# Two PSUM tiles in place of one for the score maxima of a mixture-of-experts and attention kernel, and more of the maxima beside the second layers

## The chip, the cores and the metric

The kernel runs on one core of a Trainium2 chip. The core has TensorE (matrix products, written to PSUM, a memory of 8 banks of 512 fp32 values in each of 128 partitions), VectorE, ScalarE and GpSimd (elementwise work and reductions), SyncE (here it starts most DMAs) and its DMA engines. The metric is the device time of one execution in microseconds.

## The reference

Two blocks read the same normalised input and are added to the input.

```python
x = A_x                                  # 1 x 2048 x 448
xn = layernorm(x)
return x + A(xn) + B(xn)

def A(x):                                # 16 query heads, one key and value head, Dh = 28
    q = (x @ wq).reshape(...)            # 16 heads of 28
    k, v = x @ wk, x @ wv                # 2048 x 28
    p = softmax(q k^T * 28 ** -0.5)
    return (p v) @ wo

def B(x):                                # 8 experts, each token uses 2
    gates = softmax(x @ wg); top 2, weights normalised over the two
    h = gelu(x @ w1[e])                  # 448 -> 1792
    y = h @ w2[e]                        # 1792 -> 448
    return the weighted sum over the two experts
```

For a stable softmax the kernel needs, for each query and head, the maximum of its scores over the 2048 keys. That maximum is taken ahead of the attention, while the experts run.

## The kernel before, in words

**Order of the work.** First come the norms, the projections and the gate; then the eight experts, sorted by how many tokens they have (capacities of 576 to 512, CAPS, line 25); then the attention. Expert 1 (e = 0 in the code) has its own loop (lines 1077 to 1172). Experts 2 to 8 (e = 1 to 7, lines 1224 to 1374) are the ones that the change is about. In their part the order of TensorE's instructions is the order of the program; the queues of the other engines are laid out by a scheduler, which puts the work marked as high priority first.

**An expert.** Its tokens' rows are gathered and turned by TensorE transposes (turn_x, line 268: four transposes into one PSUM bank, then two ScalarE copies out of it, then two GpSimd subtractions for the low halves). Every fp32 operand is split into a high and a low part, and a product is three products of these. The first layer (first_layer, line 1241) goes over 14 half pieces of w1 with 22 matrix products each, 11 into either half of a bank; ScalarE applies the gelu. In the second layer (lines 1286 to 1360) TensorE's rows are used as four groups of 32: in each of four phases there are 14 x 3 = 42 steps of four products (line 1338), one per row group, into the accumulators acc[0] to acc[3]; phases are parted by a drain of TensorE (line 1331). acc[0] and acc[1] are the one-bank tiles ps_w, acc[2] and acc[3] the halves of the two-bank tile ps_s2. At the end four copies (lines 1353 to 1360), alternately by ScalarE and VectorE, take the accumulators out; the turned rows of the next expert (two sets at the start of the layer, two or three at its end) and, for experts 2 to 5, the products of the tokens beyond 512 (line 1367) follow.

**The maxima.** A unit is one query tile of 128, one head and two blocks of 512 keys that lie 1024 keys apart. Units 0 to 447 cover query tiles 2 to 15. Its maximum is taken from two products: D (D_of, line 1188), queries times the difference of the two key blocks, and B (B_of, line 1198), queries times the second block. max(a, b) = relu(a - b) + b: ScalarE writes the Relu of D to a buffer (line 1322), and VectorE adds B, in place, and reduces by the maximum (pair_max, line 1203). There are two places for units:

- A burst in the first layer (pair_burst, line 1205; called from due, line 1231, ahead of the third product of a half piece's second half): two units by D and B in the four-bank tile ps_s, and a third one by its two key blocks in the tile ps_s2, reduced by VectorE at once (line 1220). Experts 2 to 7 have 8 bursts in 14 calls, expert 8 has 10. Where a call has no burst, it may finish a query tile (s_last, line 132).
- A round in the second layer (maxima, line 1310): D of two new units into banks 0 and 1 of the tile ps_s (ps in the code), and B of the two units of the round before into banks 2 and 3; then the two Relus of the new units and the two maxima of the old ones. The Relus go to two pairs of buffers in turn, RR: the two halves of cp, or two buffers gf. A round is issued before the first step and after steps 8, 17, 25, 34 and 42 of every phase, as long as the queue has units. Experts 2 to 7 take 40 units here (20 rounds of new units and one for the last maxima), expert 8 takes the rest.

The pool of these tiles is psM (line 892): ps_s with four banks, ps_s2 with two, ps_w0 and ps_w1 with one each, which fills PSUM. Expert 1 uses ps_s as well, in s_burst (line 151): up to seven units of another form, four of them reduced in one instruction of VectorE from the four banks (line 179); and turn_first (line 781) and first_scores (line 1038) put single sets there.

Of the kernel before, what the change touches and what calls it, by code (L numbers as in the profile page):

```python
# [86 lines left out]
def moe_attention(ctx, tc, x, wq, wk, wv, wo, wg, w1, w2, out, hp=200, slow=0.4, first=0.9, fin=11, find=4):  # L87
    nc = tc.nc
# [62 lines left out]
    def s_burst(b0, n):  # L151


        p, p2 = bank["s"]()
        p3 = other_psum() if n > 6 else None
        for i in range(n):
            t, c, g, j = (b0 + i) // 64, (b0 + i) // 16 % 4, (b0 + i) // 4 % 4, (b0 + i) % 4
            if (b0 + i) % 64 == 32 and t + 1 < NT:
                s_query(t + 1)
            r = slice(32 * j, 32 * j + DH)  # L160
            k = i - (n > 6)
            nc.tensor.matmul(p3 if k < 0 else p[:, k, :] if k < 4 else p2[:, k - 4, :], SQ[t][r, g, :],
                             kT4[r, c * 512:(c + 1) * 512], start=True, stop=True)
        cp = mp.tile([128, 2, 512], F32, name="cp", bufs=1)
        with tc.high_priority(offset=hp):
            parts = [(0, p3[:, None, :])] if n > 6 else []
            k = len(parts)
            parts.append((k, p[:, 0:min(n, 4)]))
            if n - k > 4:
                nc.scalar.activation(cp[:, 0:n - k - 4], p2[:, 0:n - k - 4], AF.Copy)  # L170
                parts.append((k + 4, cp[:, 0:n - k - 4]))
            red = None
            for k, q in parts:

                o, m = (b0 + k) % 192, q.shape[1]
                l = min(m, 192 - o)
                for o, a, z in ((o, 0, l), (0, l, m)):
                    if a < z:
                        r = V.tensor_reduce(MX[0][:, o:o + z - a], q[:, a:z], axis=AX.X, op=OP.max)
                        if red:  # L180
                            order(r.ins, red)
                        red = r.ins.name
# [99 lines left out]
    with ExitStack() as p0:  # L282
# [498 lines left out]
        def turn_first(i):  # L781
# [3 lines left out]
            if i < 2:  # L785
                p = psP.tile([128, 512], F32, name="ps_t", bufs=3)
            else:
                p = (psM.tile([128, 4, 512], F32, name="ps_s", bufs=1) if i % 2 == 0 else s2_psum())[:, 0]
            p = GT[i] = p.rearrange("p (c n) -> p c n", c=4)[:, :, 0:n]
# [130 lines left out]

    bank["s"] = lambda: (psM.tile([128, 4, 512], F32, name="ps_s", bufs=1), s2_psum())
    bank["s"]()
# [115 lines left out]
    def first_scores():  # L1038

        p = bank["s"]()[0]  # L1040
        mm = products([p[:, j] for j in range(4)], att["q"], 0)
        trail.append(mm.ins.name)
        P = att["P"] = att["p"].tile([128, 4, 512], F32, name="Pf", bufs=1)
        for j in range(0, 4, 2):
            order(nc.scalar.activation(P[:, j:j + 2], p[:, j:j + 2], AF.Exp, scale=SCALE).ins, trail[-1])

# [158 lines left out]
    def pair_burst():  # L1205
        u = UD[0]
        UD[0] += 3
        p, p2 = bank["s"]()
        D_of(u, p[:, 0])
        D_of(u + 1, p[:, 1])  # L1210
        ask(u + 2)
        key_of(u + 2, 0, p2[:, 0])
        B_of(u, p[:, 2])
        B_of(u + 1, p[:, 3])
        key_of(u + 2, 1, p2[:, 1])
        cp = mp.tile([128, 2, 512], F32, name="cp", bufs=1)
        m = pair_at(u + 2)[-1]
        with tc.high_priority(offset=hp):
            nc.scalar.activation(cp, p[:, 0:2], AF.Relu)
            V.tensor_reduce(MX[0][:, m:m + 1], p2.rearrange("p a b -> p (a b)"), axis=AX.X, op=OP.max)  # L1220
            for k in range(2):
                pair_max(u + k, cp[:, k], p[:, 2 + k])

    for e in range(1, E):
# [6 lines left out]
        def due(e=e):  # L1231
            k = slots[0]
            slots[0] += 1
            n = 10 if e == E - 1 else 8
            if (k + 1) * n // 14 > k * n // 14:
# [49 lines left out]

        ps = psM.tile([128, 4, 512], F32, name="ps_s", bufs=1)
        for i, *a in XS:
            turn_x(e + 1, i, *X[e + 1], *a, ps[:, 2 + i])
        XS = []
# [10 lines left out]

        until = UD[0] + 40 if e + 1 < E else NU
        queue = list(range(UD[0], until, 2))
# [7 lines left out]
        def maxima():  # L1310
# [4 lines left out]
            for j in range(4):  # L1315
                for u, what, o in ((old, B_of, 2), (new, D_of, 0)):
                    if u is not None and u % 4 // 2 == j // 2:
                        what(u + j % 2, ps[:, o + j % 2])
            with tc.high_priority(offset=hp):
                for k in range(2):  # L1320
                    if new is not None:
                        nc.scalar.activation(ra[k], ps[:, k], AF.Relu)  # L1322
                for k in range(2):
                    if old is not None:
                        pair_max(old + k, rb[k], ps[:, 2 + k])
            old = new

        maxima()
        for ph in range(4):
            if ph:  # L1330
                nc.tensor.drain()
            for f in range(NF):
                a, b = (w[:, f % 2, :] for w in W2[e, f // 2])
                for i, (l, w) in enumerate(((0, a), (1, a), (0, b))):
# [5 lines left out]
                    step = f * 3 + i + 1  # L1340
                    if step in (8, 17, 25, 34, 42):
                        if step < 42:
# [6 lines left out]
        for k, (i, *a) in enumerate(XS):  # L1349
            turn_x(e + 1, i, *X[e + 1], *a, ps[:, k])  # L1350
        r = sum(CAPS[:e])
        YY = [GP[0].tile([128, 2, 512], F32, name="yy", tag="g0", bufs=7) for _ in range(2)]
        for k in range(4):
            y = YY[k // 2][:, k % 2, 0:D]
            with tc.high_priority(offset=hp):
                if k % 2:
                    V.tensor_copy(y, acc[k][:, 0:D])
# [344 lines left out]
```

## Time and profile before

| | us |
|---|---|
| median of 3 runs (lowest, highest) | 1604.8 (1598.74, 1606.59) |
| the profiled execution | 1602.6 |
| its span, first to last instruction | 1600.9 |
| TensorE busy in the span | 1401.8 (88%) |
| ScalarE busy | 1014.8 (63%) |
| VectorE busy | 887.3 (55%) |
| GpSimd busy | 622.9 (39%) |
| second layer of expert 2: from, to | 243.7, 306.3 |
| second layers of experts 3 to 7, length | 62.2 to 62.8 |
| attention, from 1064 to 1600 | 536.0, TensorE busy 519.8 |

The profile is one execution. A line of the timeline has the start in us, the duration in us, the engine, the line of the program, the operation, what it writes and reads by the program's names (ps_s stands for every tile whose name begins so, ps_s2 among them), the shapes and how many such instructions were merged; in brackets stand the engine's idle time before it and what ended it. Lines of waits have the waiting group, whom it waited for, the total in us, the number of times and the longest. Lines of groups have the busy time and the mean in ns behind the bar, then idle time. PE is TensorE (PEld its weight loads), ACT ScalarE, DVE VectorE and POOL GpSimd.

### The profile page before, as it was taken

The page shows a single profiled execution, that of the slowest core. Times are in us where ns is not written, and L with a number is a line of the kernel's source. Part 1 is how long each engine was busy: PE and PEld are TensorE (multiplying, and loading weights), DVE is VectorE, ACT ScalarE, POOL GpSimd, SP SyncE. Part 2 cuts the span into 40 slices and gives each one's busy share as a digit, 9 for nine tenths or more (in the row PEclk, how much of TensorE's full clock was granted, in tenths as well). Part 3 has the DMA queues.
Part 4 walks back from the last instruction along what each step waited for, and adds up shares of the span by engine and source line. Part 5 has one row for each costly group of instructions (what it writes and reads, how often), then busy time and mean ns, then how long its engine had stood idle before and what let it go on. Part 6 is the DMA issues. An engine that isn't in the chain of part 4 may idle for free. (4 is left out here: it accounts for less than half of the span.)

```text
span 1600.9 us, 35307 instructions
## 1 busy us (share of the span) xinstructions
PE 1401.8 (88%) x14325; PEld 990.5 (62%) x14325; DVE 887.3 (55%) x1655; ACT 1014.8 (63%) x1275; POOL 622.9 (39%) x556
## 2 busy tenths in 40 slices
PE   7989997797698788779779779789999999999997
PEld 6877786586576567668668668554444444444443
DVE  7888873363444436337337338446555555555554
ACT  6645564365355446347447446449798999899985
POOL 7244483175157138118218217101432243224323
PEclk9999999899999989999999999999999999999999
DMA  8931241133023124114114113211121212111211
GB/s 261 306 110 39 61 135 49 55 96 91 27 80 115 33 65 133 40 43 135 47 55 135 47 55 98 51 57 32 43 67 49 55 44 67 49 54 45 67 38 37
DMA packets 103331, 122.72 MB, mean 77 GB/s; under 512 B 15298, under 2 KB 91506, under 8 KB 103038
## 3 DMA queue, kind: packets, MB, share of 16 engines
q1 hardware_dynamic: 98078, 104.11, 21.7%
q0 software_dynamic: 5088, 16.32, 3.8%
q8 instruction: 114, 1.87, 0.5%
q14 instruction: 51, 0.42, 0.1%
HBM read 96.67 MB, written 23.72 MB: 75 GB/s over the span
## 5 line engine op out<-in xcount | busy, mean ns | idle before, releaser
L1510 ACT ACTIVATE P<-ps_s 128x1536 f32<-128x1536 f32 x255 | 356.1, 1449 | 45.2 <-PE ps_s L1034 45.2
L1203 DVE CUSTOM_DVE_ANT_0 cp<-ps_s,cp 128x512 f32<-128x512 f32 x254 | 164.9, 686 | 179.9 <-ACT gf L1322 172.2
L1338 PE MATMUL ps_s<-w2h,gg 32*128 32x448 f32 x1568 | 250.9, 378 | 2.0 <-issue 1.0
L1540 PE MATMUL ps_s<-P,vaug 128*32 128x512 f32 x2040 | 249.2, 602 | 1.9 <-DVE P L1525 0.9
L1338 PE MATMUL ps_w<-w2h,g 32*128 32x448 f32 x1568 | 247.2, 375 | 1.0
L228 POOL TENSOR_TENSOR w1l<-st,w1h 128x1024 fp32r<-128x1024 f32 x49 | 120.7, 2464 | 266.8 <-ACT w1h L61 266.3
L76 PE MATMUL ps_w<-xeh,w1h 128*128 128x256 f32 (+2 forms) x896 | 170.4, 302 | 5.2 <-ACT gf L1256 4.9
L1338 PEld LDWEIGHTS ps_s<-w2h,gg 32*128 32x128 f32 x1568 | 162.0, 192 | 7.1 <-issue 6.3
L1196 PE MATMUL ps_s<-kT,qs 28*128 28x512 f32 x506 | 111.0, 456 | 60.9 <-DVE mx L1203 60.9
L1338 PEld LDWEIGHTS ps_w<-w2h,g 32*128 32x128 f32 x1568 | 160.1, 192 | 3.7 <-issue 3.1
L1322 ACT ACTIVATE gf<-ps_s 128x512 f32<-128x512 f32 x136 | 74.0, 596 | 136.2 <-PE ps_s L1191 98.4
L1338 PE MATMUL ps_s<-w2l,gg 32*128 32x448 f32 x784 | 155.4, 372 | 0.0
L1191 PE MATMUL ps_s<-kd,qs 28*128 28x512 f32 x390 | 99.7, 503 | 61.2 <-DVE mx L1203 49.4
L1338 PE MATMUL ps_w<-w2l,g 32*128 32x448 f32 x784 | 153.2, 370 | 0.0
L76 PEld LDWEIGHTS ps_w<-xeh,w1h 128*128 128x128 f32 x896 | 132.9, 192 | 32.4 <-issue 21.6
L1203 DVE CUSTOM_DVE_ANT_0 gf<-ps_s,gf 128x512 f32<-128x512 f32 x136 | 88.6, 689 | 114.0 <-ACT cp L1322 113.2
L1220 DVE TENSOR_REDUCE mx<-ps_s 128x1 f32<-128x1024 f32 x58 | 70.8, 1221 | 145.5 <-PE ps_s L1196 145.5
L1322 ACT ACTIVATE cp<-ps_s 128x512 f32<-128x512 f32 x138 | 75.0, 595 | 120.4 <-PE ps_s L1196 100.7
L76 PE MATMUL ps_w<-xeh,w1l 128*128 128x256 f32 (+2 forms) x896 | 149.9, 290 | 0.0
L1034 PEld LDWEIGHTS ps_s<-qah,kT 29*128 29x128 f32 x1024 | 72.5, 183 | 122.5 <-issue 77.7
L1548 DVE TENSOR_TENSOR o<-ps_s,o 128x512 f32<-128x512 f32 x111 | 76.8, 691 | 122.7 <-PE ps_s L1540 122.7
L1034 PE MATMUL ps_s<-qah,kT 29*128 29x512 f32 x1024 | 138.0, 457 | 3.9 <-DVE o L1548 3.7
(316 smaller groups left out, 3129.1 us busy)
## 6 DMA issues: line engine op xcount, KB each, us to landing
st<-in_B_w_dram SPq DMA_DIRECT2D x56, 448.0 KB
st<-in_B_w_dram SPq DMA_DIRECT2D x52, 384.0 KB
st<-in_B_w_dram SPq DMA_DIRECT2D x104, 64.0 KB
y_d<-yy SPq DMA_DIRECT2D x28, 224.0 KB
xn_d<-xn SPq DMA_DIRECT2D x16, 256.0 KB
rb<-s_d SPq DMA_DIRECT2D x15, 256.0 KB
xn<-in_A_x_dram SPq DMA_DIRECT2D x16, 224.0 KB
qs<-qh_d SPq DMA_DIRECT2D x64, 56.0 KB
```

The lines of the kernel that those rows point to most:

```text
L76: yield nc.tensor.matmul(out, a, b, start=i == 0, stop=i == n - 1)
L228: (nc.gpsimd if e else V).tensor_tensor(b, st, a.bitcast(F32), op=OP.subtract)
L1034: mm = nc.tensor.matmul(ps[j], k[r, ks], q[r].rearrange("p h q -> p (h q)"), start=i == 0, stop=i == 2)
L1191: nc.tensor.matmul(bank, q, KD[0][r, c * 512:c * 512 + 512], start=True, stop=True)
L1196: nc.tensor.matmul(bank, q, kT4[r, o:o + 512], start=True, stop=True)
L1203: V.tensor_tensor_reduce(d, b, d, 1.0, -3.0e38, OP.add, OP.max, MX[0][:, m:m + 1])
L1220: V.tensor_reduce(MX[0][:, m:m + 1], p2.rearrange("p a b -> p (a b)"), axis=AX.X, op=OP.max)
L1322: nc.scalar.activation(ra[k], ps[:, k], AF.Relu)
L1338: mm = nc.tensor.matmul(acc[k][:, 0:D], gate(k, f, l)[r], w[r], start=ph == f == i == 0, stop=ph == 3 and f == NF - 1 and i == 2)
L1510: nc.scalar.activation(out, in_, AF.Exp, scale=SCALE)
L1540: nc.tensor.matmul(p[32 * g:32 * g + 32, :], vaug[:, 2 * kp + k, :], P[k, g], start=i == 0, stop=i == 1)
L1548: V.tensor_tensor(o, p, o, op=OP.add)
```

## The change

The tile ps_s of four banks becomes two tiles of two banks, ps_a and ps_b. In bursts and rounds ps_a holds the products D, which ScalarE reads, and ps_b the products B, which VectorE reads. The sets of transposes at the start of a second layer go one to either tile, those at its end to ps_a, ps_b and ps_a. acc[0] and acc[1] are taken out by ScalarE, acc[2] and acc[3] by VectorE. In s_burst of expert 1 the reduction of four banks becomes two of two banks.

Units move: experts 2 to 7 have 6 bursts in place of 8 and 46 units in the second layer in place of 40; expert 8 has 8 bursts in place of 10 and takes the remaining 40 units, in place of 34, in its second layer. Rounds are issued after every seventh step (six in a phase in place of five).

```diff
@@ s_burst
-        p, p2 = bank["s"]()
+        pa, pb, p2 = bank["s"]()
...
-            parts.append((k, p[:, 0:min(n, 4)]))
+            parts += [(k, pa[:, 0:min(n, 2)])] + [(k + 2, pb[:, 0:min(n, 4) - 2])] * (n > 2)
...
+    def halves_psum():
+        return [psM.tile([128, 2, 512], F32, name=f"ps_{n}", bufs=1) for n in "ab"]
+
-    bank["s"] = lambda: (psM.tile([128, 4, 512], F32, name="ps_s", bufs=1), s2_psum())
+    bank["s"] = lambda: (*halves_psum(), s2_psum())
@@ pair_burst
-        p, p2 = bank["s"]()
-        D_of(u, p[:, 0])
-        D_of(u + 1, p[:, 1])
+        pa, pb, p2 = bank["s"]()
+        D_of(u, pa[:, 0])
+        D_of(u + 1, pa[:, 1])
...
-        B_of(u, p[:, 2])
-        B_of(u + 1, p[:, 3])
+        B_of(u, pb[:, 0])
+        B_of(u + 1, pb[:, 1])
...
-            nc.scalar.activation(cp, p[:, 0:2], AF.Relu)
+            nc.scalar.activation(cp, pa, AF.Relu)
...
-                pair_max(u + k, cp[:, k], p[:, 2 + k])
+                pair_max(u + k, cp[:, k], pb[:, k])
@@ due
-            n = 10 if e == E - 1 else 8
+            n = 8 if e == E - 1 else 6
@@ the second layer
-        ps = psM.tile([128, 4, 512], F32, name="ps_s", bufs=1)
+        ps = halves_psum()
         for i, *a in XS:
-            turn_x(e + 1, i, *X[e + 1], *a, ps[:, 2 + i])
+            turn_x(e + 1, i, *X[e + 1], *a, ps[i][:, 0])
...
-        until = UD[0] + 40 if e + 1 < E else NU
+        until = UD[0] + 46 if e + 1 < E else NU
@@ maxima
-                for u, what, o in ((old, B_of, 2), (new, D_of, 0)):
+                for u, what, o in ((old, B_of, 1), (new, D_of, 0)):
                     if u is not None and u % 4 // 2 == j // 2:
-                        what(u + j % 2, ps[:, o + j % 2])
+                        what(u + j % 2, ps[o][:, j % 2])
...
-                        nc.scalar.activation(ra[k], ps[:, k], AF.Relu)
+                        nc.scalar.activation(ra[k], ps[0][:, k], AF.Relu)
...
-                        pair_max(old + k, rb[k], ps[:, 2 + k])
+                        pair_max(old + k, rb[k], ps[1][:, k])
@@ the steps and what follows them
-                    if step in (8, 17, 25, 34, 42):
+                    if step % 7 == 0:
...
         for k, (i, *a) in enumerate(XS):
-            turn_x(e + 1, i, *X[e + 1], *a, ps[:, k])
+            turn_x(e + 1, i, *X[e + 1], *a, ps[k % 2][:, k // 2])
...
-                if k % 2:
+                if k > 1:
                     V.tensor_copy(y, acc[k][:, 0:D])
```

turn_first and first_scores take their banks from the new tiles in the same way.

More of the change, by code (lines that the diff above doesn't have):

```diff
@@ L161, in s_burst @@
             k = i - (n > 6)
-            nc.tensor.matmul(p3 if k < 0 else p[:, k, :] if k < 4 else p2[:, k - 4, :], SQ[t][r, g, :],
+            nc.tensor.matmul(p3 if k < 0 else (pa, pb, p2)[k // 2][:, k % 2, :], SQ[t][r, g, :],
                              kT4[r, c * 512:(c + 1) * 512], start=True, stop=True)
@@ L787, in turn_first @@
             else:
-                p = (psM.tile([128, 4, 512], F32, name="ps_s", bufs=1) if i % 2 == 0 else s2_psum())[:, 0]
+                p = (psM.tile([128, 2, 512], F32, name="ps_a", bufs=1) if i % 2 == 0 else s2_psum())[:, 0]
             p = GT[i] = p.rearrange("p (c n) -> p c n", c=4)[:, :, 0:n]
@@ L1038, in first_scores @@
     def first_scores():
-        p = bank["s"]()[0]
-        mm = products([p[:, j] for j in range(4)], att["q"], 0)
+        ps = halves_psum()
+        mm = products([ps[j // 2][:, j % 2] for j in range(4)], att["q"], 0)
         trail.append(mm.ins.name)
@@ L1044, in first_scores @@
         for j in range(0, 4, 2):
-            order(nc.scalar.activation(P[:, j:j + 2], p[:, j:j + 2], AF.Exp, scale=SCALE).ins, trail[-1])
+            order(nc.scalar.activation(P[:, j:j + 2], ps[j // 2], AF.Exp, scale=SCALE).ins, trail[-1])
     one, two = (split_w1, load_w1), (split_w2, load_w2)
@@ L1284, in moe_attention @@
             open_attention()
-        ps = psM.tile([128, 4, 512], F32, name="ps_s", bufs=1)
+        ps = halves_psum()
         for i, *a in XS:
-            turn_x(e + 1, i, *X[e + 1], *a, ps[:, 2 + i])
+            turn_x(e + 1, i, *X[e + 1], *a, ps[i][:, 0])
         XS = []
```

## The prediction

> **What bounds the kernel now.** I read the stretches by engine first, in which TensorE is the busiest everywhere, then the waits inside one second layer (expert 2's, from 243.7 to 306.3 us), and then single rounds in the timeline. The waits of that layer, columns: total us, times, longest:
>
> ```profile
> DVE cp L1203 <- ACT gf L1322: 26.1, 10, 9.7
> ACT gf L1322 <- PE ps_s L1191: 17.8, 9, 2.2
> ACT cp L1322 <- PE ps_s L1196: 16.5, 9, 2.0
> DVE gf L1203 <- ACT cp L1322: 16.4, 9, 1.9
> ```
>
> The strange ones are the first and the last. VectorE's maximum that works in place on cp waits for ScalarE's Relu into gf, and the one on gf for the Relu into cp. The code hands the two buffers over from round to round: the maximum of a round reads the Relu of the round before. So no data is passed in the waits named here; all that the two share in a round is the PSUM tile ps_s, ScalarE in banks 0 and 1, VectorE in banks 2 and 3. One round, engine by engine:
>
> ```profile
> 301.00 0.50 PE L1191 MATMUL ps_s<-kd,qs 28*128 28x512 f32 x2 [1.02 <-DVE mx L1203]
> ...
> 301.31 0.36 PE L1338 MATMUL ps_w<-w2h,g 32*128 32x448 f32 x1
> ...
> 302.98 0.38 PE L1338 MATMUL ps_s<-w2h,gg 32*128 32x448 f32 x2
> 304.14 0.50 PE L1196 MATMUL ps_s<-kT,qs 28*128 28x512 f32 x2 [0.78 <-DVE mx L1203]
> ```
> ```profile
> 301.56 1.09 ACT L1322 ACTIVATE cp<-ps_s 128x512 f32<-128x512 f32 x2 [2.04 <-PE ps_s L1196]
> ```
> ```profile
> 302.68 0.69 DVE L1203 CUSTOM_DVE_ANT_0 gf<-ps_s,gf 128x512 f32<-128x512 f32 x1 [1.82 <-ACT cp L1322]
> ```
>
> Products at 301.00, Relus 0.56 later, maxima 1.12 later (0.03 after the Relus' end at 302.65), next products 1.46 later: 3.14 us a round, one engine after the other. The steps of the layer between them (four products each) start at 301.31, and the ninth at 302.98: 0.21 a step. They are done before the maxima are, and TensorE idles 0.78 to 1.02. The chain bounds the second layers, not TensorE.
>
> That a whole tile is guarded, not its banks, shows a second time at the layer's start, where two transposes go to banks 2 and 3 and the first products to banks 0 and 1:
>
> ```profile
> 236.03 0.31 PE L76 MATMUL ps_w<-xeh,w1h 128*128 128x320 f32 x1
> 236.27 0.50 PE L1191 MATMUL ps_s<-kd,qs 28*128 28x512 f32 x2
> 236.27 0.73 PE L1196 MATMUL ps_s<-kT,qs 28*128 28x512 f32 x4
> 236.93 0.42 PE L76 MATMUL ps_w<-xeh,w1h 128*128 128x320 f32 x1
> 237.19 0.60 PE L76 MATMUL ps_w<-xel,w1h 128*128 128x320 f32 x3
> 237.63 0.75 PE L76 MATMUL ps_w<-xeh,w1l 128*128 128x320 f32 x4
> 239.62 0.63 PE L271 MATMUL ps_s<-ident,xs 128*128 128x128 f32 x4 [1.24 <-ACT gf L1256]
> 241.42 1.11 PE L271 MATMUL ps_s<-ident,xs 128*128 128x128 f32 x4 [1.18 <-ACT xs L276]
> 243.71 0.79 PE L1191 MATMUL ps_s<-kd,qs 28*128 28x512 f32 x2 [1.18 <-ACT xs L276]
> ```
> ```profile
> 240.78 0.59 ACT L276 ACTIVATE xs<-ps_s 128x512 f32<-128x512 f32 x1
> ```
> ```profile
> 239.43 0.08 DVE L1203 DVE_READ_ACCUMULATOR2_ANT mx<- 128x1 f32 x1
> ```
>
> Each waits until ScalarE has read another bank of the tile; and the first transposes (the profile names ScalarE) start 0.11 after VectorE ends the last burst's maxima.
>
> **The change part by part.**
>
> *Rounds.* With a tile for each reader, nothing orders the maxima behind the Relus of their own round. What is then late next? The path over VectorE alone stands at the layer's end, where a last round holds only products that VectorE reads:
>
> ```profile
> 307.29 0.49 PE L1196 MATMUL ps_s<-kT,qs 28*128 28x512 f32 x2 [1.01 <-DVE mx L1203]
> 309.19 0.77 PE L271 MATMUL ps_s<-ident,xs 128*128 128x128 f32 x4 [1.41 <-DVE mx L1203]
> ...
> 313.98 0.74 PE L1367 MATMUL ps_w<-w2h,gg 128*128 128x448 f32 x1
> 314.52 0.57 PE L1367 MATMUL ps_w<-w2l,gg 128*128 128x448 f32 x1
> ...
> 319.75 0.42 PE L1367 MATMUL ps_w<-w2l,gg 128*128 128x448 f32 x1
> ```
>
> 1.90 us from products to the next use of their banks. ScalarE's path is 0.56 + 1.09 + 0.11 (the gap between VectorE's end and the transposes above, taken for it too) = 1.76. TensorE's own pace with a round every 7 steps is at least 0.31 + 7 x 0.21 = 1.78, and at most the present 8-step round less its wait and a step, 3.14 - 1.02 - 0.21 = 1.91. All three are close, so they will sometimes add up: I take 2.0, bounds 1.90 and 2.15. At the three changes of phase TensorE drains:
>
> ```profile
> 278.99 0.50 PE L1196 MATMUL ps_s<-kT,qs 28*128 28x512 f32 x2 [0.61 <-DVE mx L1203]
> ```
>
> The wait is 0.41 shorter than the 1.02 of other 8-step rounds, so a drain costs 0.4; there I take 2.2. That both engines read PSUM at once costs nothing: in a burst they do so now, from 194.43 and 194.47 on, and VectorE's 1024 elements in 1.23 are no slower than 2048 in 2.29 where it reads alone (the reduction of expert 1, below).
>
> ```profile
> 194.43 1.03 ACT L1219 ACTIVATE cp<-ps_s 128x1024 f32<-128x1024 f32 x1 [1.07 <-PE ps_s L1196]
> ```
> ```profile
> 194.47 1.23 DVE L1220 TENSOR_REDUCE mx<-ps_s 128x1 f32<-128x1024 f32 x1 [3.78 <-PE ps_s L1196]
> ```
>
> ScalarE also makes three copies for the next weights in the layer:
>
> ```profile
> L61 ACT ACTIVATE w1h<-st 128x1024 fp32r<-128x1024 f32 x3 | 3.2, 1060 | 0.0
> ```
>
> They lie in its idle 2 us now; in a 2.0 us round it idles 0.91, so each delays a round by 0.15: 0.5 a layer.
>
> Now the count. 46 units make 23 rounds and a 24th with maxima alone; the 24th call is at step 35 of the last phase, so 7 steps follow. 20 x 2.0 + 3 x 2.2 + 0.31 + 7 x 0.21 + 0.5 = 48.9. Before: from 243.71 to 306.2, where the last steps end:
>
> ```profile
> 306.32 0.54 ACT L1359 ACTIVATE yy<-ps_w 128x448 f32<-128x448 f32 x1 [0.52 <-PE ps_w L1338]
> ```
>
> 62.5 - 48.9 = 13.6, for six experts 81.6. The eighth expert's layer:
>
> ```profile
> 1004.66 0.49 PE L1191 MATMUL ps_s<-kd,qs 28*128 28x512 f32 x2 [1.52 <-DVE mx L1203]
> ```
> ```profile
> 1063.81 0.55 ACT L1359 ACTIVATE yy<-ps_w 128x448 f32<-128x448 f32 x1 [7.18 <-PE ps_s L1338]
> ```
>
> 59.1 now. Its 40 remaining units make 20 cycles, the last call at step 14 of the last phase: 17 x 2.0 + 3 x 2.2 + 0.31 + 28 x 0.21 = 46.8, gain 12.3. Rounds together: 93.9.
>
> *Start of a layer.* The first transposes go into the tile that only ScalarE reads, so they need not wait for VectorE (1.24), the second go into the other tile, and the first products wait for the first transposes' copies only: these end at 240.78 + 0.59 = 241.37 now, 240.13 if all of the 1.24 is gained. So 2.3 to 3.5 of the time up to 243.71 goes; ScalarE's other work stands between, I take 2.9, six times: 17.4. The eighth expert has no transposes and loses its wait of 1.52: 18.9 together.
>
> *End of a layer.* Expert 2 now waits from 306.2 for the last lone round (309.19) and three sets of transposes in turn until 313.98: 7.8. Then the lone round lies 7 steps (1.5 us) ahead of the end, the first two sets follow at once, and only the third waits for ScalarE: two output copies (0.54 each), two copies of the first set (0.59 each, 1.09 as a pair), the gap 0.11, the transposes (0.63): 3.0 with 0.1 to begin. Gain 4.8, experts 2 to 4: 14.4. Of the other three I take expert 6, with two sets:
>
> ```profile
> 825.66 0.55 ACT L1359 ACTIVATE yy<-ps_w 128x448 f32<-128x448 f32 x1 [0.53 <-PE ps_w L1338]
> ```
> ```profile
> 831.57 0.78 PE L76 MATMUL ps_w<-xeh,w1h 128*128 128x256 f32 x2
> ```
>
> 5.9, then 1.5 (two sets at 0.7 each); 4.4 three times, 13.2. VectorE's taking both output copies of the s2 tile is within these, off the path. Together 27.6.
>
> *The clock.* After this gap TensorE's products start every 0.37 (14 of them from 314.52 to 319.75), not every 0.21: 2.3 us lost in each of three experts; for the other three I estimate half, as fewer dense products follow at once. At 239.62 the transposes still take 0.63, at 241.42, 3.0 after the last dense product ended (237.63 + 0.75 = 238.38), 1.11: a gap under 3 us seems harmless. The new gaps are 1.5 to 3.0, one of them at the edge: I take 8 of 10.5. [...]
>
> *Bursts.* The first layers give up 14 bursts. Around one, the products start at 236.03 and go on at 236.93, against a pitch of (237.63 - 237.19)/3 = 0.15: 0.75 each, 10.5. TensorE is busy all around it; if GpSimd's subtractions held the stage, half of this would stay.
>
> *Expert 1.* Its 21 reductions of four banks
>
> ```profile
> L179 DVE TENSOR_REDUCE mx<-ps_s x21: 2277/2291/2293, 98.9 to 188.1; 128x4 f32<-128x2048 f32 x21
> ```
>
> become two of 1.23, 0.17 more each, 0 to 3.5 in all; most is hidden by products: 1 lost.
>
> *Sum.* 93.9 + 18.9 + 27.6 + 8 + 10.5 - 1 = 157.9. The profiled execution took 1602.6 (span 1600.9); it would take 1444.7. The median of the runs, 1604.8, is 2.2 above it: 1446.9, say 1447.
>
> **The rivals.** *TensorE sets the pace.* If entering a round costs what the present waits leave (1.91, and 2.12 + 0.41 - 0.21 = 2.32 at a drain) and its in-order queue then adds the engines' lateness, a round takes 2.13 and 2.5: 20 x 0.13 + 3 x 0.3 = 3.5 more a layer, 25 in seven, and with the clock's 8 gone 1480. For it: the three paths lie within 0.15 us. Against: the first number counts the pipeline's filling, which a queue without waits doesn't pay.
>
> *Still in turn.* If the maxima wait for ScalarE for another reason than the tile, the layer keeps 3.14 a round and has three more: 23 x 3.14 + 1.78 = 74.0, 11.5 more, six times; 20 x 3.14 + 6.2 = 69.0 in the last, 9.9 more; less 10.5 of bursts: 68 slower, 1673. It decides from a round of (62.5 + 1.5 - 1.8)/23 = 2.7 on. For it: the buffers cp and gf pass between the same engines. Against: the waits name the other buffer, and the transposes show the same guard without them. [...] The rows (0.03 us after the Relus' end) speak for a guard by tile.
>
> **How the numbers follow.** Forecast 0.76, TensorE's pace 0.15, still in turn 0.08; 0.01 for gains and losses that cancel. The forecast's own ends: rounds of 1.90 and 2.1, starts of 3.5 and the whole clock, 22 less; 2.15, ends 1 us later, no clock and half the bursts, 45 more. So 1424 to 1492, with the first rival inside. A measurement of this kernel tells about 0.5% from no change; faster by more than that 0.91, within 0.01, slower 0.08.
>
> **What would show it.** Right: maxima that start within 0.1 us of the Relus, rounds 1.9 to 2.1 apart, waits of VectorE for ScalarE (L1203 for L1322) near zero, second layers of 49 us. Wrong: rounds over 2.7, or first layers that grow by what the second lose.

## The result, and the profile after

| | us |
|---|---|
| before, median of 4 runs beside the changed kernel (lowest to highest) | 1604.3 (1598.7 to 1606.6) |
| changed, median of 4 runs | 1474.9 (1474.2 to 1477.7) |
| ratio, 95% interval | 0.920 (0.918 to 0.923) |
| profiled execution of changed, its span, TensorE clock | 1474.7, 1472.9, 0.976 |

The profiled executions differ by 1602.6 - 1474.7 = 127.9 us; 157.9 were forecast. The chain that bounded the second layers is gone. Two rounds of the changed kernel (timeline: start, length; ScalarE, then VectorE):

```profile
264.19 1.09 ACT L1325 ACTIVATE gf<-ps_a 128x512 f32<-128x512 f32 x2 [0.59 <-PE ps_a L1194]
266.48 1.09 ACT L1325 ACTIVATE cp<-ps_a 128x512 f32<-128x512 f32 x2 [1.21 <-PE ps_a L1194]
```
```profile
264.53 0.69 DVE L1206 CUSTOM_DVE_ANT_0 cp<-ps_b,cp 128x512 f32<-128x512 f32 x1 [0.70 <-PE ps_b L1199]
266.55 0.69 DVE L1206 CUSTOM_DVE_ANT_0 gf<-ps_b,gf 128x512 f32<-128x512 f32 x1 [0.70 <-PE ps_a L1194]
268.57 0.69 DVE L1206 CUSTOM_DVE_ANT_0 cp<-ps_b,cp 128x512 f32<-128x512 f32 x1 [0.71 <-PE ps_b L1199]
```

Maxima and Relus of a round run side by side, and VectorE's maxima are 2.02 apart. The waits of expert 2's second layer (243.5 to 294.2; total us, times, longest) name TensorE where they named ScalarE:

```profile
DVE cp L1206 <- PE ps_b L1199: 12.5, 11, 4.2
...
DVE gf L1206 <- PE ps_a L1194: 6.1, 9, 0.7
...
ACT gf L1325 <- POOL gg L1270: 1.6, 1, 1.6
```

The rows that bound the stages of expert 3 follow: the end of the layer before it (an output copy), then TensorE's transposes, the extra tokens' products, the first and last products of the first layer, the first round.

```profile
294.12 0.98 ACT L1362 ACTIVATE yy<-ps_w 128x448 f32<-128x448 f32 x2 [2.13 <-PE ps_w L1341]
```
```profile
294.21 0.65 PE L271 MATMUL ps_a<-ident,xs 128*128 128x128 f32 x4
...
296.13 0.43 PE L271 MATMUL ps_a<-ident,xs 32*128 32x32 f32 x4 [0.84 <-ACT xs L276]
296.50 0.47 PE L1370 MATMUL ps_w<-w2h,gg 128*128 128x448 f32 x1
296.80 0.36 PE L1370 MATMUL ps_w<-w2l,gg 128*128 128x448 f32 x1
297.01 0.36 PE L1370 MATMUL ps_w<-w2h,gg 128*128 128x448 f32 x1
...
302.28 0.64 PE L76 MATMUL ps_w<-xeh,w1h 128*128 128x256 f32 x4
...
352.95 0.69 PE L76 MATMUL ps_w<-xeh,w1l 128*128 128x288 f32 x4
...
355.52 0.50 PE L1194 MATMUL ps_a<-kd,qs 28*128 28x512 f32 x2
```

The same three rows of the kernel before:

```profile
322.44 0.64 PE L76 MATMUL ps_w<-xeh,w1h 128*128 128x256 f32 x4
...
369.69 0.69 PE L76 MATMUL ps_w<-xeh,w1l 128*128 128x288 f32 x4
...
375.37 0.79 PE L1191 MATMUL ps_s<-kd,qs 28*128 28x512 f32 x2 [1.18 <-ACT xs L276]
```

End of a layer (output copy to first product): 8.2 instead of 16.1. First layer (first product to the end of the last): 353.64 - 302.28 = 51.4 instead of 370.38 - 322.44 = 47.9, longer with two bursts less. Start (to the first round): 1.9 instead of 5.0. All experts, read in this way and added up, with the second layer from its first round to its output copy:

| us gained | forecast | measured |
|---|---|---|
| second layers, experts 2 to 8 (before 434.3, changed 357.3) | 93.9 | 77.0 |
| starts, experts 2 to 8 (32.9, 11.3) | 18.9 | 21.6 |
| ends and clock, experts 3 to 8 (71.5, 33.2) | 35.6 | 38.3 |
| first layers, experts 3 to 8 (286.7, 295.6) | 9.0 | -8.9 |
| expert 1 and the first layer of 2 (ends at 238.4, 241.8) | 0.5 | -3.4 |
| behind the last second layer (537.1, 533.8) | 0 | 3.3 |
| sum | 157.9 | 127.9 |

So two terms failed: the second layers by 17, the first layers by 18 (22 with expert 1 and expert 2's). The 3.3 behind the last second layer were not forecast, and their cause is open; in the kernels below this stretch takes 533.3 to 536.0. The waits of ScalarE and TensorE in expert 3's first layer, before and then changed, show who holds it:

```profile
ACT gf L1256 <- POOL gg L1267: 6.4, 3, 3.0
...
ACT w1h L61 <- DMA st<-in_B_w_dram: 0.5, 1, 0.5
```
```profile
PE ps_w L76 <- ACT gf L1256: 1.0, 1, 1.0
```
```profile
ACT gf L1259 <- POOL gg L1270: 8.9, 5, 3.2
...
ACT w1h L61 <- DMA st<-in_B_w_dram: 3.5, 2, 1.8
```
```profile
PE ps_w L76 <- ACT gf L1259: 4.6, 3, 2.2
```

TensorE waits 4.6 instead of 1.0 for gelus, these for GpSimd to have read their buffer, and the weights' high halves for weights that have not come. TensorE is not busy all around a burst, as the forecast had it.

Some of TensorE's clock goes too. Expert 5's first layer before and then changed (the stretch, its length, the busy time and number of instructions of TensorE, its weight loads, VectorE, ScalarE and GpSimd, then the granted clock, the DMA engines' share and their GB/s):

```profile
585.13:633.19 48.06, 46.76 (x359) 41.68 (x357) 31.83 (x45) 32.68 (x52) 37.62 (x27) 1.00 0.36 105
```
```profile
526.72:579.48 52.76, 48.27 (x349) 43.93 (x348) 28.02 (x35) 30.97 (x50) 38.55 (x29) 0.94 0.33 97
```

The granted clock of the first layers of experts 3 to 8 was 1.00, 1.00, 1.00, 1.00, 0.96 and 0.93 before, and is 0.97, 0.93, 0.94, 0.96, 0.93 and 1.00 in the changed kernel. An estimate from these clocks and the lengths: 13.6 us of full clock are missing instead of 5.5, so up to 8 of the 18 may have come this way, behind TensorE's waits.

### The profile page after: what moved, and what is told of

Read it like the earlier page. It is cut to its first block, busy times and chain, and to the rows that moved or that the text cites. A ratio compares the mean times of both kernels' runs of the same rounds, so it can differ in the third digit from the quotient of the medians.

```text
span 1472.9 us, 35255 instructions
## 1 busy us (share of the span) xinstructions
PE 1384.3 (94%) x14325; PEld 979.7 (67%) x14325; DVE 887.0 (60%) x1690; ACT 1020.5 (69%) x1303; POOL 624.5 (42%) x556
## 5 line engine op out<-in xcount | busy, mean ns | idle before, releaser
L1206 DVE CUSTOM_DVE_ANT_0 cp<-ps_b,cp 128x512 f32<-128x512 f32 x252 | 163.7, 687 | 98.0 <-PE ps_b L1199 76.6
L1341 PEld LDWEIGHTS ps_w<-w2h,g 32*128 32x128 f32 x1568 | 164.3, 185 | 5.9 <-issue 3.2
L1341 PE MATMUL ps_w<-w2l,g 32*128 32x448 f32 x784 | 167.0, 368 | 0.0
L1341 PE MATMUL ps_s<-w2l,gg 32*128 32x448 f32 x784 | 166.5, 366 | 0.0
L1456 POOL TENSOR_TENSOR o<-o,rb 128x512 f32<-128x512 f32 x15 | 19.4, 1294 | 308.7 <-DMA rb<-s_d 308.7
L1223 DVE TENSOR_REDUCE mx<-ps_s 128x1 f32<-128x1024 f32 x44 | 53.7, 1220 | 152.9 <-PE ps_s L1199 152.9
L1543 PEld LDWEIGHTS ps_s<-P,vaug 128*32 128x32 f32 x2040 | 54.0, 109 | 131.7 <-issue 79.0
L1513 ACT ACTIVATE P<-P 128x1024 f32<-128x1024 f32 (+1 forms) x128 | 135.5, 1059 | 0.0
L1206 DVE CUSTOM_DVE_ANT_0 gf<-ps_b,gf 128x512 f32<-128x512 f32 x152 | 99.4, 689 | 58.7 <-PE ps_a L1194 37.8
L1325 ACT ACTIVATE gf<-ps_a 128x512 f32<-128x512 f32 x152 | 83.4, 596 | 72.8 <-PE ps_a L1194 39.4
```

What stands on the lines that cost most here:

```text
L1206: V.tensor_tensor_reduce(d, b, d, 1.0, -3.0e38, OP.add, OP.max, MX[0][:, m:m + 1])
L1325: nc.scalar.activation(ra[k], ps[0][:, k], AF.Relu)
L1341: mm = nc.tensor.matmul(acc[k][:, 0:D], gate(k, f, l)[r], w[r], start=ph == f == i == 0, stop=ph == 3 and f == NF - 1 and i == 2)
L1456: nc.gpsimd.tensor_tensor(o, o, rb, op=OP.mult)
L1513: nc.scalar.activation(out, in_, AF.Exp, scale=SCALE)
L1543: nc.tensor.matmul(p[32 * g:32 * g + 32, :], vaug[:, 2 * kp + k, :], P[k, g], start=i == 0, stop=i == 1)
```

## The experiments

Two theories of the missing 30 us were set against each other. Q: the bursts of a first layer come at other places in VectorE's queue, ahead of its copies of weights, and delay the weights. G: GpSimd has too much to do between two gelus, wherever the bursts lie. In the table, stages are summed as above (first layers and ends: experts 3 to 8; the others: 2 to 8); each median is of four runs (odd slots: five) and each ratio to the kernel before on the same chip (1603.4 to 1604.3). The stages are read from one profile per kernel.

| kernel | us | ratio (95%) | first | second | start | end |
|---|---|---|---|---|---|---|
| changed | 1474.9 | 0.920 (0.918 to 0.923) | 295.6 | 357.3 | 11.3 | 33.2 |
| tiles alone | 1426.7 | 0.891 (0.887 to 0.894) | 281.9 | 315.0 | 11.2 | 38.8 |
| counts alone | 1664.4 | 1.037 (1.033 to 1.040) | 291.1 | 515.2 | 32.1 | 47.4 |
| early bursts | 1473.6 | 0.918 (0.915 to 0.921) | 263.9 | 391.1 | 9.6 | 33.1 |
| w1 low on VectorE | 1457.5 | 0.908 (0.905 to 0.911) | 287.2 | 349.7 | 11.3 | 33.1 |
| last subtractions on VectorE | 1464.3 | 0.914 (0.911 to 0.918) | 290.6 | 344.1 | 17.4 | 33.2 |
| all three of these | 1435.5 | 0.897 (0.893 to 0.900) | 261.6 | 355.1 | 9.6 | 33.2 |
| tiles, last subtractions | 1416.5 | 0.883 (0.879 to 0.886) | 286.2 | 299.8 | 18.1 | 38.8 |
| tiles, 34 units, 10 bursts | 1452.2 | 0.905 (0.901 to 0.909) | 323.0 | 301.8 | 11.3 | 33.1 |
| tiles, a burst in slot 2 | 1453.9 | 0.907 (0.903 to 0.910) | 309.0 | 315.0 | 11.3 | 38.9 |
| tiles, last subtr., expert 8's slots | 1418.0 | 0.884 (0.880 to 0.887) | 281.4 | 300.7 | 18.8 | 38.8 |
| 34 units, no burst in slot 2 | 1464.8 | 0.915 (0.912 to 0.917) | 330.4 | 304.4 | 11.3 | 33.2 |
| tiles, last subtr., odd slots | 1402.2 | 0.874 (0.872 to 0.876) | 272.1 | 296.6 | 15.1 | 40.4 |

**The two halves of the change.** Tiles alone, against the changed kernel (the transposes and output copies stay as in the change):

```diff
-            n = 8 if e == E - 1 else 6
+            n = 10 if e == E - 1 else 8
...
-        until = UD[0] + 46 if e + 1 < E else NU
+        until = UD[0] + 40 if e + 1 < E else NU
...
-                    if step % 7 == 0:
+                    if step in (8, 17, 25, 34, 42):
```

> The two tiles alone, with the counts of before: 8 bursts (10 in expert 8) in a first layer, 40 units in a second, a round after steps 8, 17, 25, 34 and 42. Two theories of the 30 us that were missed. Theory Q (the queue of VectorE): in the changed kernel the first burst of a first layer comes one slot later, the copy of the first swift w2 piece stands behind it on VectorE, the staging buffer comes free 2 to 3 us later, and so on down to the gelu and TensorE; the number of bursts isn't the cause, their places are. With the places of before the first layers of experts 3 to 7 take 47.7, 47.7, 47.8, 44.1 and 46.0 us again (51.1, 50.6, 52.5, 46.6 and 48.9 in the changed kernel) and that of expert 8 its 51.8 (44.1 changed). Theory G (GpSimd has too much to do between two gelus since the layers became shorter): they stay at 50 to 52, with two bursts more. Both: no wait of VectorE for ScalarE in the second layers. If TensorE's own pace sets the rounds (2.015 us measured for 7 steps, so 0.545 for the products of a round at 0.21 a step), a second layer takes 35.3 + 20 x 0.545 + 1.2 of drains + 1.4 of a late second round = 49; if the engines that read PSUM set it, 45. Time: Q 1435 to 1460, G 1460 to 1485.

It took 1426.7: the tiles alone gain 177 us, and the other half of the change gives 48 of them back. That is 8 under the lower end of theory Q's range. First layers are about those of before again (47.8, 48.0, 47.8, 44.3, 44.3, and 49.8 in expert 8), as theory Q says. Second layers take 45.0, 45.1, 46.2, 44.9, 44.8 and 46.2, so the products of a round don't hold TensorE for 0.545, and the 2.02 of the changed kernel is not its pace. VectorE's costliest waits in expert 3's second layer (343.2 to 388.4) follow, and none of its waits there names ScalarE:

```profile
DVE gf L1206 <- PE ps_b L1199: 10.1, 8, 4.3
```


Counts alone is the kernel before with the minus lines of this diff, its four banks one tile.

> The counts alone: 46 units in a second layer, a round after every 7 steps, 6 bursts (8 in expert 8) in a first layer, the maxima's four banks still one tile. If it is the tile that makes VectorE wait, rounds stay at 3.13 us and a second layer of 23 of them takes 62.2 + 3 x 3.13 + 1.8 = 73.4, 11 more, six times, and 9 more in expert 8's (20 rounds instead of 17): 1604 + 77 = 1681; with theory Q's first layers (3 to 4 longer from the places of the bursts, 7.6 shorter in expert 8) 1693, with bursts worth 0.75 each 1671. Rival (the new places of the rounds, one after every 7 steps, are what lets them run at 2.0): 1475 to 1500.

1664.4; rounds of 3.13 and second layers of 74.3. The waits of one of them (249.6 to 323):

```profile
DVE cp L1203 <- ACT gf L1322: 26.7, 11, 8.5
...
DVE gf L1203 <- ACT cp L1322: 20.2, 11, 1.9
```

VectorE waits for ScalarE's Relu into the other buffer again. So the tile is the cause, and the more frequent rounds are not. The time is 7 under the lowest of the three (1671) that were expected if the tile makes VectorE wait. With the one tile, too, the first layers of experts 3 to 7 get longer with two bursts less (by 0.6 to 1.4, expert 6's by 7.6), and the first copy of w2 comes 10.6 us after expert 3's first product; so this does not need the two tiles, though it is less in four of the five layers.

**Slots, VectorE's queue and GpSimd's.** A first layer has 14 slots for bursts: slot 0 and the odd ones up to 11 in the pieces of the first token half, the even ones from 2 and slot 13 in those of the second. Straight behind each piece of the second half the program asks for weights, and the first four requests, behind slots 2, 4, 6 and 8, each have VectorE copy one piece of w2 and subtract it, in program order behind a burst of that slot. Six bursts lie in slots 2, 4, 6, 9, 11 and 13, eight in 1, 3, 5, 6, 8, 10, 12 and 13. Early bursts moves the six:

```diff
-            if (k + 1) * n // 14 > k * n // 14:
+            if (k in (1, 3, 5, 8, 10, 12)) if n == 6 else ((k + 1) * n // 14 > k * n // 14):
```

> The changed kernel with the same six bursts of a first layer in slots 1, 3, 5, 8, 10 and 12 instead of 2, 4, 6, 9, 11 and 13 (experts 2 to 7; expert 8 as it is). Theory Q: the first w2 copy on VectorE starts some 7.7 us after the layer's first product instead of 10.6, the waits of ScalarE for staged weights go, and the first layers of experts 3 to 7 fall by 3 to 5 us each, to 46 to 48; with expert 2's 15 to 30 us in all: 1445 to 1460. Theory G: same work on GpSimd, so no change: 1472 to 1478.

The first layers did fall by 5 to 8 us, to 45.1, 45.0, 45.0, 42.3 and 42.2, but the second layers grew to 55 to 58: 1473.6, no change in all. Both theories failed on a half: Q had the first layers right and the total wrong, G the total right (1472 to 1478) and the first layers wrong. Where it went (end of expert 3's first layer; GpSimd, then ScalarE):

```profile
363.09 0.45 POOL L279 TENSOR_TENSOR xeh<-xs,xeh 64x128 fp32r<-64x128 f32 x1 [1.46 <-DMA xs<-xn_d,tokp]
363.82 0.87 POOL L249 DMA_INDIRECT xs<-xn_d,tokp  x1 [0.28 <-POOL xeh L279]
364.75 1.54 POOL L1270 TENSOR_TENSOR gg<-gf,gg 128x512 fp32r<-128x512 f32 x2
```
```profile
366.32 0.60 ACT L1325 ACTIVATE gf<-ps_a 128x512 f32<-128x512 f32 x1 [6.08 <-POOL gg L1270]
```

The gelu's low half is made by GpSimd behind two gathers and the next expert's transposed tokens, one of which waits for a DMA; until then the second Relu of the second layer can't write the buffer gf. Counted from the layer's first product the subtraction ends at 58.7 here and at 59.0 in the changed kernel: TensorE was earlier, GpSimd wasn't.

W1 low on VectorE and last subtractions on VectorE each take a piece of GpSimd's queue away:

```diff
-        (nc.gpsimd if e else V).tensor_tensor(b, st, a.bitcast(F32), op=OP.subtract)
+        (nc.gpsimd if e and pc < 3 else V).tensor_tensor(b, st, a.bitcast(F32), op=OP.subtract)
```

> The changed kernel with the low halves of w1's pieces 3 to 6 (four subtractions of 128x1024, 2.4 us each on GpSimd, in each first layer) made by VectorE. Theory G: GpSimd loses 10 of its 39 us of a first layer, the gelus no longer wait for its subtractions, first layers fall to TensorE's 46 and the late second round of the second layers (3.4 to 5.2 us instead of 2.0) comes earlier: 1430 to 1450. Theory Q: VectorE's queue holds the w2 copies back longer still, staged weights come later: first layers as long or longer, 1472 to 1490.

```diff
-                nc.gpsimd.tensor_tensor(gg[:, :, o:o + w], g[:, :, i], gg[:, :, i].bitcast(F32), op=OP.subtract)
+                (V if hf and pc > 4 else nc.gpsimd).tensor_tensor(gg[:, :, o:o + w], g[:, :, i], gg[:, :, i].bitcast(F32), op=OP.subtract)
```

> The changed kernel with the subtractions of the last two pieces of a first layer (pieces 5 and 6 of the second token half) made by VectorE, which is idle there. Theory G (GpSimd's queue): the second round's Relu no longer waits for the read of its buffer gf, and the second and third rounds of the layers of experts 2 to 7 fall from 3.4 to 5.2 us to 2.0 to 2.5; first layers, which GpSimd's earlier subtractions hold, lose 0 to 2. Six times 1.4 to 3.2, so 8 to 20 in all: 1455 to 1467. Rival (the late round comes from ScalarE's own copies and gelus at the layer's start): the round stays at 3.4 or more, 1472 to 1478.

The first gave 1457.5, between the theories: the first layers of experts 3 to 5 fell to 47.2 to 47.5, so GpSimd's load has a share in them; those of 6 and 7 rose to 49.5 and 51.4 (why these two is open), and the second round stayed late. The second gave 1464.3, in the range of theory G. Its effect on expert 2's second round, in the changed kernel and then here:

```profile
249.27 0.60 ACT L1325 ACTIVATE gf<-ps_a 128x512 f32<-128x512 f32 x1 [1.61 <-POOL gg L1270]
```
```profile
248.38 1.09 ACT L1325 ACTIVATE gf<-ps_a 128x512 f32<-128x512 f32 x2 [0.59 <-PE ps_b L1199]
```

Second layers are 49.1 to 49.4 in experts 2 to 5. Some of it is lost at the start of experts 6 and 7 (5.0 and 4.5 instead of 2.0). All three together:

> The changed kernel with three things together: the six bursts of a first layer in slots 1, 3, 5, 8, 10 and 12, the low halves of w1's pieces 3 to 6 and the last two pieces' subtractions on VectorE. Alone, the early bursts made the first layers 6 us shorter and the second round of the second layers that much later, since the last subtraction still came at 58 us from the layer's first product. Theory G: GpSimd's 48 us of work between a layer's first product and that subtraction are what held both; relieved of 10 + 4 of them, first layers keep 44 to 46 and second layers fall to 48.5 to 49.5: six times 5 + 2 less, 1425 to 1440. Theory Q (the order on VectorE alone): the added subtractions on VectorE push its w2 copies back, first layers return to 48 to 51: 1455 to 1475.

1435.5, in theory G's range: first layers of 44.3 and 42.3, as short as with the early bursts alone, and this time the second layers pay less for it. They stay at 50 to 52, where 48.5 to 49.5 had been expected, for a new reason, in VectorE's queue:

```profile
244.07 0.99 DVE L1270 TENSOR_TENSOR gg<-gf,gg 128x512 fp32r<-128x512 f32 x2 [4.63 <-ACT gg L61]
245.95 0.69 DVE L1206 CUSTOM_DVE_ANT_0 cp<-ps_b,cp 128x512 f32<-128x512 f32 x1 [0.89 <-PE ps_b L1199]
```

The moved subtraction waits 4.6 us for ScalarE, and the first round's maxima stand behind it.

**From the tiles alone.** The same edit for the last subtractions, on the tiles alone:

> The tiles alone with the counts of before (1426.7) and the last two pieces' subtractions on VectorE: the second round, now 4.3 us, falls to 2.0 to 2.2, and the second layers from 44.6 to 42.4; expert 8's is as it was. Six times 2.2: 1410 to 1416. If ScalarE's own work makes the round late: 1424 to 1430.

And 34 units in place of 40, on the tiles alone:

```diff
-            n = 10 if e == E - 1 else 8
+            n = 12 if e == E - 1 else 10
...
-        until = UD[0] + 40 if e + 1 < E else NU
+        until = UD[0] + 34 if e + 1 < E else NU
```

> The tiles with still fewer pairs in the second layers: 34 units there, 10 bursts (12 in expert 8) in the first layers, rounds after steps 8, 17, 25, 34 and 42. Three rounds less in a second layer that TensorE sets take 3 x 0.29 = 0.9 less (so much per round is left of 44.5 - 2.3 of the late round - 1.2 of drains - 168 x 0.21, in 20 rounds); two bursts more in a first layer cost 1.0 to 1.4 each by the first layers of the early bursts against those of the tiles alone, (47.5 - 44.7)/2 and (44.0 - 42.0)/2; or 0.75 each by the pitch before. Six times 0.6 to 1.9 more, and 1 to 4 in expert 8: 1431 to 1442. If a round in a second layer costs the 2.0 us of the changed kernel, 6 less a layer: 1400 to 1410.

The subtractions gave 1416.5, half a microsecond over the range: the second layers are 15.2 shorter, the starts 6.9 longer, and expert 6's first layer 4.7 longer. In that layer TensorE waits once for 1.95 us; in the kernel with expert 8's slots moved, whose code for expert 6 is the same, it takes 44.1 instead of 49.0. So a single layer of one profile can be 5 us off. The 34 units took 1452, above every forecast: second layers of 43 as expected, first layers of 49.9 to 54.8 (58.8 in expert 8). Ten bursts lie in slots 1, 2, 4 and on, so slot 2 was suspected, and in the tiles alone one burst was moved to it from slot 1, all else equal:

```diff
-            if (k + 1) * n // 14 > k * n // 14:
+            if (k in (2, 3, 5, 6, 8, 10, 12, 13)) if n == 8 else ((k + 1) * n // 14 > k * n // 14):
```

> The tiles alone with one burst of each first layer of experts 2 to 7 moved by one slot, from 1 to 2 (slots 2, 3, 5, 6, 8, 10, 12 and 13), counts as before. Theory Q: the first copy of a w2 piece on VectorE stands behind the burst of slot 2 and starts 10.5 us after the layer's first product instead of 7.6, and the first layers rise by 3 to 4 us, to 50 to 52 (experts 3, 4, 5), with the number of bursts unchanged: six times 3 to 4 over the 1426.7 of the tiles alone, 1444 to 1452. If the number of bursts or GpSimd's sum of work is the cause and the slot is not: 1424 to 1430.

1453.9, 2 over theory Q's range: 27 us for one burst in each of six layers, one slot later. First product and first copy of w2 in expert 3, tiles alone and then with slot 2:

```profile
293.61 0.64 PE L76 MATMUL ps_w<-xeh,w1h 128*128 128x256 f32 x4
```
```profile
301.25 0.62 DVE L992 CAST w2h<-st 128x896 fp32r<-128x896 f32 x1
```
```profile
300.67 0.64 PE L76 MATMUL ps_w<-xeh,w1h 128*128 128x256 f32 x4
```
```profile
310.62 0.69 DVE L1206 CUSTOM_DVE_ANT_0 cp<-ps_b,cp 128x512 f32<-128x512 f32 x1
...
311.23 2.38 DVE L992 CAST w2h<-st 128x896 fp32r<-128x896 f32 x1
```

7.6 and 10.6 us after the first product: the copy stands behind the burst's last maximum. The changed kernel has it at 312.83 - 302.28 = 10.6 (its row stands in the last section). First layers rise to 51.4, 51.3, 51.9, 53.5 and 49.3. Two tries to use this missed, one on the tiles with the last subtractions moved and one on the 34 units:

```diff
-            if (k + 1) * n // 14 > k * n // 14:
+            if (k in (1, 3, 4, 5, 6, 8, 10, 11, 12, 13)) if n == 10 else ((k + 1) * n // 14 > k * n // 14):
```

> The tiles alone with the last two pieces' subtractions on VectorE (1416.5), and expert 8's ten bursts in slots 1, 3, 4, 5, 6, 8 and 10 to 13, none in slot 2. Theory Q: its first layer, 49.6, falls to 46 or 47: 3 us, 1411 to 1415. Otherwise 1415 to 1419.

```diff
-            if (k + 1) * n // 14 > k * n // 14:
+            if (k in (1, 3, 4, 5, 6, 8, 9, 10, 12, 13)) if n == 10 else k not in (0, 2):
```

> 34 units and 10 bursts as tried, 1452, but no burst in slot 2 (slots 1, 3, 4, 5, 6, 8, 9, 10, 12 and 13; expert 8's twelve in all but 0 and 2). Theory Q: first layers fall from 54 to 49.5 to 50.5 (the 47.5 of eight bursts and 1.0 to 1.4 for each of two more), second layers stay at 43: 1425 to 1436. If the number of bursts is the cause: 1447 to 1456.

1418.0 and 1464.8: the layers concerned (expert 8's in the first kernel, all in the second) had the first copy at 7.6 to 7.7, but a burst in slot 4, and there the second copy came at 17.3 to 17.8 instead of 13.8 to 14.2. Slot 4 lies ahead of a copy just as slot 2 does. So, on the tiles with the last subtractions moved, with every such slot free:

```diff
-            if (k + 1) * n // 14 > k * n // 14:
+            if k in ((0, 1, 3, 5, 7, 9, 10, 11, 12, 13) if n == 10 else (1, 3, 5, 7, 9, 11, 12, 13)):
```

> The tiles alone with the last two pieces' subtractions on VectorE (1416.5), and no burst in slots 2, 4, 6 or 8, which lie straight ahead of VectorE's copies of w2 pieces in program order (odd slots, and the free ones from 9 on; expert 8 slot 0 too). The kernels with expert 8's burst out of slot 2 alone, and with 34 units, had left or put bursts in slot 4, and there the second copy started at 17.4 to 17.8 us instead of 14.1. Theory Q: all four copies start at 7.6, 14, 20.5 and 27; expert 8's first layer falls from 49.9 to 45 to 47; those of experts 2 to 7, which TensorE holds at 47.4 and 44.0 already, lose 0 to 1.2 each: 1404 to 1414. If the slots don't matter beyond the first copy: 1414 to 1420.

1402.2, the fastest of all and 2 under theory Q's range. The layer's first product and the four copies in expert 3:

```profile
296.01 0.64 PE L76 MATMUL ps_w<-xeh,w1h 128*128 128x256 f32 x4
```
```profile
303.65 0.62 DVE L992 CAST w2h<-st 128x896 fp32r<-128x896 f32 x1
310.18 0.62 DVE L992 CAST w2h<-st 128x896 fp32r<-128x896 f32 x1
316.57 0.62 DVE L992 CAST w2h<-st 128x896 fp32r<-128x896 f32 x1
322.96 0.62 DVE L992 CAST w2h<-st 128x896 fp32r<-128x896 f32 x1
```

7.6, 14.2, 20.6 and 27.0, to 0.1 as expected. Expert 8's first layer falls from 49.9 to 45.6, those of experts 3 to 5 from 47.7 to 46.2, that of expert 6 from 49.0 to 43.8 (most of it the 5 us above), and second layers take 42 to 43. In the kernel without free slots the third and fourth copies of expert 3's layer came at 24.2 and 31.5, behind bursts in slots 6 and 8. The granted clock is 1.00 in all six first layers.

So theory Q holds for the first layers, with a share of GpSimd's, and theory G for the second round of the second layers.

## Why the prediction was right, and where it wasn't

*The cause* was right. The counts alone behave as the rival "still in turn" was priced (74.0 a layer forecast, 74.3 measured; 1673, and 1664); the tiles alone end it. With two tiles ScalarE and VectorE read their banks side by side, in the same 1.09 and 0.69 as before. In the one-tile kernels it is the order by tile that makes one wait for the other: rounds of 3.13 with the counts alone, of 2.02 with the same counts and two tiles.

*The rounds* were right: 2.0 forecast, 2.02 measured, 1.32 of two maxima and the 0.70 from their end to the next start, in the bracket of that row. Of the signs named, the waits of VectorE for ScalarE are gone; maxima start 0.07 from the Relus in one of the rounds shown and 0.34 in the other, where 0.1 was named; second layers of experts 2 to 7 take 50.4 to 53.1, where 49 was. The layer was mis-sized, 51.0 on average instead of 48.6. The missing cost is mainly the second round: its Relu needs the buffer gf, which GpSimd's subtraction must have read, and the forecast looked at the paths over VectorE, ScalarE and TensorE alone. Last subtractions on VectorE brings 13.2 of the 17 back (344.1, where 340.2 was forecast), and 6.1 of that is lost at the starts. Expert 8's layer, 48.7 instead of 46.8, keeps its 1.9; why is open.

*Starts and ends* came out 2.7 us better each, and the clock there did come back: from expert 2's output copy to the next first product it was 0.68 before and is 1.00. The extra tokens' products start 0.20 apart behind the new gap (296.80, 297.01), not 0.37. My sum had 8 of the clock's 10.5; with the whole 10.5 the ends are 27.6 + 10.5 = 38.1, and 38.3 was measured. How close the two come is in part luck: the ends of experts 2 to 4 gained 22.9 where 21.3 follow from the sum, those of 5 to 7 15.4 where 16.8 do.

*The bursts* are the step that failed: "TensorE is busy all around it; if GpSimd's subtractions held the stage, half of this would stay." Not half but less than nothing stayed. Fewer bursts also lie in other slots, the first of them ahead of VectorE's copy of w2. That copy and its subtraction free the staging buffer, whose next weights ScalarE and then GpSimd split, before GpSimd comes to the subtraction that frees the gelu's buffer. The two ends of this chain are shown, the slot by experiment and TensorE's wait by the rows; the steps between are read from the program and the waits. One slot is worth 27 us at equal counts; 10.5 had been forecast for all the bursts. The price of 0.75 itself holds where no burst stands in slots 2, 4 and 6: from odd slots (eight bursts) to early bursts (six) the first layers of experts 3 to 5 fall from 46.2 to 45.0, those of 6 and 7 from 43.9 to 42.2, so 0.6 and 0.8 for each burst. Against the tiles alone it looks like (47.8 - 45.1)/2 = 1.4, but these have a burst in slot 6. In the early bursts the second layer pays it back, waiting for GpSimd.

*What was not asked* is whether each half of the change pays. My own terms had the answer: with 20 rounds in 168 steps TensorE needs 20 x 0.31 + 168 x 0.21 = 41.5 and three drains of 0.4, 42.7 (42.0 to 42.3 measured in experts 2 to 6 with odd slots), against 48.9 with 23; two bursts at 0.75 are no match for 6 us. By the same sum a round of seven steps gives TensorE 1.78 of work, less than the 2.02 of VectorE's path, so it waits; 20 rounds leave 41.5/20 = 2.1 for each, and VectorE's path is hidden. I priced only the pair.

That the median, 1474.9, lies inside the range of 1424 to 1492 is luck in part: the slow end was made of longer rounds, longer ends, no gain of clock and half of the bursts, and what came was a late second round and longer first layers. It also lies near the 1480 of the rival in which TensorE sets the pace, for other reasons than the rival's: rounds took 2.02 and not 2.13, and the clock was kept at the ends and lost in the first layers.

Open: whether 34 units and 10 bursts pay when no burst lies ahead of a copy, and why the starts of experts 6 and 7 are late with VectorE's subtractions; neither was tried. An estimate for the first, from odd slots: expert 8's layer with ten such bursts takes 45.6, those of experts 6 and 7 with eight 43.9, so two bursts cost 1.7, and three rounds less save TensorE 3 x 0.31 = 0.9.

## What to carry to other kernels

When a change unties a dependency and moves work at once, price the two parts apart: here the first gave 177 us and the second took 48. Work that is moved or thinned out also changes its place in each engine's queue; look for the small copy behind it that frees a buffer, and follow that buffer to the engine that waits last. When a wait is said to be hidden behind other work, check it for every engine that holds the buffer, in the stage where it counts.

## What the runs showed of the hardware that was not expected

*The clock falls without a long gap.* In the kernel with a burst in slot 2, TensorE's only idle times between 322 and 325 us, by the timeline, are 0.56 and 0.73, and yet the granted clock falls to 0.50 for more than three microseconds (stretches of 1 us; columns as in the section on the result, the clock third from the end):

```profile
322.99 0.49 PE L1199 MATMUL ps_s<-kT,qs 28*128 28x512 f32 x1 [0.56 <-DVE mx L1223]
324.21 0.51 PE L1199 MATMUL ps_b<-kT,qs 28*128 28x512 f32 x2 [0.73 <-DVE mx L1206]
```
```profile
322.00:323.00 1.00, 0.43 (x3) 0.12 (x3) 1.00 (x2) 0.00 (x0) 1.00 (x2) 1.00 0.07 15
323.00:324.00 1.00, 0.48 (x1) 0.17 (x1) 1.00 (x3) 0.41 (x1) 1.00 (x2) 1.00 0.84 237
324.00:325.00 1.00, 0.79 (x4) 0.54 (x5) 0.39 (x3) 0.75 (x1) 0.44 (x1) 0.81 0.90 257
325.00:326.00 1.00, 1.00 (x5) 1.00 (x5) 1.00 (x2) 0.28 (x1) 0.00 (x0) 0.50 0.79 164
326.00:327.00 1.00, 1.00 (x6) 1.00 (x6) 1.00 (x3) 0.07 (x1) 0.00 (x0) 0.50 0.75 283
327.00:328.00 1.00, 1.00 (x6) 1.00 (x6) 0.97 (x4) 1.00 (x2) 0.00 (x0) 0.50 0.10 35
```

TensorE was about half busy for two microseconds (0.43 and 0.48 of 1 us each), with products of 28 rows. So "a gap under 3 us seems harmless" in the prediction is too kind. An estimate from the rows: 0.19 + 3 x 0.50 = 1.7 us of full clock are missing from 324 to 328, where the two waits are 1.29 together. What makes the clock fall was not shown; if it is these waits, a wait of TensorE can cost more than its own length.

*VectorE's copy and GpSimd get in each other's way, and who starts first decides.* A copy of 128x896 on VectorE takes 2.39 in the changed kernel, where it starts while GpSimd splits weights:

```profile
312.83 2.39 DVE L992 CAST w2h<-st 128x896 fp32r<-128x896 f32 x1
```
```profile
312.35 2.40 POOL L228 TENSOR_TENSOR w1l<-st,w1h 128x1024 fp32r<-128x1024 f32 x1 [1.80 <-ACT w1h L61]
```

It ends 0.47 behind GpSimd's instruction (315.22, 314.75). With odd slots the copy at 303.65 takes 0.62, though GpSimd works there too, from 0.12 later on, and it is GpSimd's instruction that takes longer (1.65; the same form takes 1.28 by the median in the changed kernel where no copy or subtraction of VectorE's runs beside it):

```profile
303.77 1.65 POOL L1270 TENSOR_TENSOR g<-gf,g 128x512 fp32r<-128x512 f32 x1 [2.15 <-ACT g L61]
```

In the traces of all fourteen kernels, each of the 195 copies of w2 by VectorE that start inside a GpSimd instruction of elementwise work ends 0.48 to 0.61 behind it, and 196 of the 197 others take 0.62 to 0.63 (one takes 5.92). Why was not shown. So a copy that comes later can also last longer: behind a burst in slot 2 the first copy of expert 3 starts 2.9 later and ends 4.7 later.
